# A kernel of linear attention and a dense layer: another order for all its steps

## The chip, the cores and the metric

The kernel runs on one core of one Trainium2 chip. A core has five engines with an instruction queue each: PE (TensorE, matmuls and transposes into the PSUM memory), DVE (VectorE), ACT (ScalarE, activation functions), POOL (GpSimd) and SP (SyncE, which issues DMA transfers here). Each queue is worked through strictly in order, and engines wait for each other through semaphores. PEld is the part of PE that loads weights ahead of the matmuls. The metric is the time of one execution on the device, in microseconds (us); smaller is better.

## The reference, cut to what matters

With x of 2048 tokens by 448 features, 16 heads of 28 and an inner width of 1792 (`split` and `merge_heads` stand for the reshapes):

```python
xn = _layernorm(x, axis=-1)
return x + _A_ref(xn, A_wqkv, A_w_phi, A_wo) + _B_ref(xn, B_w1, B_b1, B_w2)

def _A_ref(x, wqkv, w_phi, wo):          # H = 16, Dh = 28
    q, k, v = split(x @ wqkv)
    pq = jnp.einsum("bhsd,hdf->bhsf", q, w_phi)
    pk = jnp.einsum("bhsd,hdf->bhsf", k, w_phi)
    phi_q = jnp.concatenate([_softmax(pq, axis=-1), _softmax(-pq, axis=-1)], axis=-1)
    phi_k = jnp.concatenate([_softmax(pk, axis=-1), _softmax(-pk, axis=-1)], axis=-1)
    kv = jnp.einsum("bhsf,bhsd->bhfd", phi_k, v)
    z  = jnp.einsum("bhsf->bhf", phi_k)
    num = jnp.einsum("bhqf,bhfd->bhqd", phi_q, kv)
    den = jnp.einsum("bhqf,bhf->bhq", phi_q, z)[..., None] + 1e-6
    return merge_heads(num / den) @ wo

def _B_ref(x, w1, b1, w2):
    h = jnp.einsum("bsd,df->bsf", x, w1) + b1
    sp = jnp.log1p(jnp.exp(-jnp.abs(h))) + jnp.where(h > 0, h, jnp.zeros_like(h))
    return jnp.einsum("bsf,fd->bsd", h * jnp.tanh(sp), w2)
```

Everything up to `kv` and `z` needs all tokens; only then can any output of the attention be made. The dense layer (`_B_ref`) needs only the normalised x and is free to lie anywhere.

## The kernel before

**One list sets the order.** The whole kernel is a table of named steps, each of which appends instructions to the queues of the engines that it uses. A string named `ORDER` (L147) lists all step names; `run_order` calls them in that order. So the place of a name in the list fixes the place of each of its instructions in the queue of its engine. Waits follow from what each instruction reads and writes (`Program.op` and `Program.resolve`); a list that is legal gives the same numbers whatever its order. An instruction that waits holds up all that stands behind it in its queue.

**Tiles and pairs.** The 2048 tokens are 16 tiles of 128; two tiles make a pair (0 to 7). Most steps are named by a letter, a pair or tile, a part and an engine letter (`d` DVE, `a` ACT, `p` POOL, `m` DMA, `b` ACT and DVE together, `t` ACT tile by tile):

- `lx0s` to `lx6s` load x (tiles 0-1, 2-3, 4-5, 6-7, 8-11, 12-15; L270), `lkm`, `lkt`, `lvm` the weights of k and v (L273, L281), `lqT0` to `lqT3` the weights of q, transposed by the DMA on the way (L285), `lpa` the feature weights, `lbs` the bias, `l1m0` to `l1m2` and `l1t` the first dense weight (L277), `l2s` the second (L305), `los` the output weight (L312). The last letter is the issuing queue, `s` for SP and `a` for ACT.
- `st` statistics of a tile (L467 and L468 on DVE, or three activations on ACT), `rs` the reciprocal deviation of a pair (on ACT, or two instructions on POOL, L473 and L476), `xn` the normalised pair (three instructions on DVE, L501; or a small shift on DVE, L489, and three instructions on POOL, L496), `xt` its transpose: on PE with a copy out of PSUM (L509, L514 for ACT and L516 for DVE), or as a DMA from SP (`m`, L521). A DMA transpose of this kind also waits until tiles 0 and 15 of x have landed.
- `wtk`, `wmk`, `wmq` fold the feature weights into the weights of k and q (L561, L585); `qd` is a DVE copy that needs all four `lqT` (L289), and `wmq` needs `qd`.
- `v`, `k`, `q` of a pair are 14 matmuls each in two halves (part 1 has 8, part 2 has 6; `pair_part`, L438). Behind the second half, `v` is copied out of PSUM (DVE or ACT), `k` and `q` leave through two exponentials on ACT, of plus and of minus (L623, L684). `e` of a tile is the DMA transpose of the exponentials of q (L692); they lie in three buffers, so that pair u+3 waits for the `e` of pair u.
- `kn` of a pair and sign: a sum and a reciprocal on DVE (L631, L633) and a multiplication on POOL (L635). `kv` of a pair adds its 16 matmuls into one bank (L652); the first starts after any pair, the last needs all. `kvz` masks the sum (L664) and turns it by a DMA.
- `f1.3` and the like are the first dense matmul, of token half 1 and chunk 3 of 14; each is 14 matmuls in two halves (also L438) and a Mish activation on ACT (L703).
- `nd` of a tile: 16 small matmuls for numerator and denominator (L726) and seven instructions on DVE (L741 to L752); `ot` the DMA transpose of the result (L761).
- `G` and `wo` of a pair: the second dense matmul and the output matmul, in halves (`pair_out`, L866); for the last pair `g14`, `g15`, `wo7F`, `wo7H` (L828, L844). The last of them adds x (`finish`, L793). `sto` and `stt` store.
- `z16` is 16 matmuls on constants at the start (`warm`, L376), `pm pp pk pi pw bd pv` fill constants on POOL; `pp` is three memsets of gaps in the buffers of q.

**PSUM** has eight banks. `take2` and `take1` hand out the pair or the bank that was used longest ago, in the order of the list; so another order also gives other banks, and other waits for the engine that empties them.

**The stretches** of the order: loads and normalisation of the first pairs; `v k q` of all pairs with `kn` beside them; six `f` and the eight `kv`; the other 22 `f` with `nd` between them; then `G` and `wo` with the last `nd`; stores at the end.

Of the kernel before, what the change touches and what calls it, by code (L numbers as in the profile page):

```python
# [168 lines left out]
def _kernel(es, nc, A_x, A_wqkv, A_w_phi, A_wo, B_w1, B_b1, B_w2, out):  # L169
    def sb(name, shape, dtype):  # L170
        return es.enter_context(nc.sbuf_tensor(name, shape, dtype))

# [94 lines left out]


    def load_x(a, b, eng):
        dma(eng, lambda e: e.dma_start(x_all[:, a:b, :], x2[:, a:b, :]), w=[("x", t) for t in range(a, b)], tag="ldx")  # L270
# [235 lines left out]
    def transpose7(e, b, src, cut=7):  # L506
        for c in range(7):
            to = bank16(b)[:, c * P:(c + 1) * P] if c < cut else bank16(b + 1)[:, (c - cut) * P:(c - cut + 1) * P]
            ins = e.transpose(to, src[:, c * P:(c + 1) * P], ident[:])  # L509
        return ins  # L510

    def evac(eng, dst, src, r, w, tag):
        if eng == "ACT":
            op("ACT", lambda e: e.activation(dst(), src(), ACT.Copy), r=r, w=w, tag=tag)  # L514
        else:
            op("DVE", lambda e: e.tensor_copy(dst(), src()), r=r, w=w, tag=tag)  # L516
# [492 lines left out]
```

## Time and profile before

| what | value |
|---|---|
| median of 3 runs | 153.88 us (153.58, 153.88, 154.25) |
| the profiled execution | 154.01 us, with a span of 152.1 us |
| granted clock of PE in it | 1.0 |
| busy: PE, DVE, ACT, POOL | 145.4, 102.4, 74.1, 41.4 us |
| DMA | 17.24 MB, mean 113 GB/s |

The span runs from the first instruction of the profile to the last; the execution's time has some 2 us more around it. The profile is one execution. Its page gives totals; the trace behind it gives a timeline for each engine, what each engine's idle time waited for, and the chain of work that ended last. In a row of a timeline the columns are the start and the length in us, engine, line of the kernel, operation, what is written and read, shape and count, and in brackets the idle time ahead of it with what ended it; instructions of one kind that follow each other are merged. "SPq" is SP's queue issuing a DMA, and the length there is that of the issue. PE is pipelined: the ends of matmuls are modelled, so the distance between starts tells more than the length. In the chain of waits, the columns are start, length and engine with line.

### The profile page before, as it was taken

To read this page: it belongs to the slowest core of one execution; us is meant where nothing else is said; L and a number is where in the kernel's file an instruction comes from. 1 tells how busy PE (TensorE), PEld (TensorE's weight loads), DVE (VectorE), ACT (ScalarE), POOL (GpSimd) and SP (SyncE) were. 2 spreads that over 40 slices of the span, in tenths; PEclk is the share of its full clock that TensorE was granted. 3 is DMA by queue.
4 is the path that set the end of the run, shared out by engine and by line. 5 is a ranking of instruction groups with operands and counts; after the bars stand their busy time and mean duration, and the time that the engine had idled before them with its cause. 6 is when DMAs were issued, how large, how long until landed. Compare 5 with 4: busy or idle time off the path is not lost.

```text
span 152.1 us, 4002 instructions
## 1 busy us (share of the span) xinstructions
PE 145.4 (96%) x1735; PEld 76.1 (50%) x1735; DVE 102.4 (67%) x224; ACT 74.1 (49%) x96; POOL 41.4 (27%) x59
## 2 busy tenths in 40 slices
PE   7799997999899999999989999999999999999993
PEld 3475543556455584445434445444555555554552
DVE  0997999999999503059998378999373377252452
ACT  3889989796979994776756387100000000000000
POOL 7704743799899970000000000000000000000000
PEclk9999999999999999999999999999999999999999
DMA  5999759989999998840913510803300016003025
GB/s 136 294 136 337 156 166 161 251 158 136 198 190 173 251 271 207 157 89 0 98 37 59 39 26 0 65 2 65 60 0 4 16 49 181 0 4 60 0 100 201
DMA packets 39997, 17.24 MB, mean 113 GB/s; under 512 B 33964, under 2 KB 39212, under 8 KB 39980
## 3 DMA queue, kind: packets, MB, share of 16 engines
q1 hardware_dynamic: 39372, 16.87, 53.5%
q8 instruction: 13, 0.21, 0.6%
q10 hardware_dynamic: 608, 0.12, 0.4%
q14 instruction: 4, 0.03, 0.1%
HBM read 7.02 MB, written 1.84 MB: 58 GB/s over the span
## 4 chain that ended last, share of the span: by engine, by line
PE 69%; DVE 18%; SPq 6%; DMA 3%; ACT 2%; issue 1%
PE PS L438 32%; PE PS L866 28%; DVE stats L467 4%; PE PS L828 3%; SPq L285 3%; DMA x_all<-in_A_x_dram 3%; DVE v_all L745 3%; DVE v_all L747 2%; PE PS L652 2%; PE PS L726 2%; DVE v_all L749 2%; DVE xn L752 2%; DVE v_all L516 1%; DVE mv L468 1%; ACT actT L684 1%
## 5 line engine op out<-in xcount | busy, mean ns | idle before, releaser
L438 PE MATMUL PS<-xnT,W 64*128 64x512 bf16 x392 | 44.9, 376 | 0.9 <-ACT actT L623 0.5
L866 PE MATMUL PS<-W,actT 64*128 64x448 bf16 x392 | 38.7, 349 | 0.0
L703 ACT ACTIVATE actT<-PS,b1T 128x1024 bf16<-128x1024 f32 x28 | 29.8, 1113 | 13.4 <-PE PS L438 13.3
L438 PEld LDWEIGHTS PS<-xnT,W 64*128 64x128 bf16 x392 | 18.9, 94 | 21.7 <-DVE v_all L747 0.9
L866 PEld LDWEIGHTS PS<-W,actT 64*128 64x128 bf16 x392 | 18.8, 94 | 17.2
L635 POOL TENSOR_TENSOR actT<-actT,rSk 128x896 bf16<-128x896 bf16 x16 | 26.6, 1702 | 1.9 <-DVE rSk L633 1.3
L793 DVE TENSOR_TENSOR x_all<-PS,x_all 128x448 bf16<-128x448 f32 (+1 forms) x16 | 9.1, 615 | 15.8 <-PE PS L866 15.1
L631 DVE TENSOR_REDUCE Sk<-actT 128x32 f32<-128x896 bf16 x16 | 16.8, 1047 | 0.2
L741 DVE COPY Sq<-PS 128x16 f32<-128x16 f32 x32 | 4.0, 167 | 17.1 <-PE PS L726 17.0
L623 ACT ACTIVATE actT<-PS 128x896 bf16<-128x896 f32 x16 | 13.7, 923 | 1.0 <-PE PS L438 0.9
L438 PE MATMUL PS<-Wpk,xnT 64*128 64x448 bf16 x112 | 12.9, 350 | 1.0 <-DVE rSk L633 0.8
L438 PE MATMUL PS<-Wkv,xnT 64*128 64x448 bf16 x112 | 12.6, 349 | 0.0
L438 PE MATMUL PS<-Wpq,xnT 64*128 64x448 bf16 x112 | 12.5, 349 | 0.0
L467 DVE BATCH_NORM_STATS2 stats<-x_all 128x6 f32<-128x448 bf16 x14 | 8.5, 607 | 4.3 <-DMA x_all<-in_A_x_dram 4.3
L749 DVE TENSOR_TENSOR v_all<-v_all 128x464 f32<-128x464 f32 x16 | 10.3, 642 | 0.6
L745 DVE TENSOR_TENSOR v_all<-PS,Sq 128x464 f32<-128x464 f32 x16 | 10.3, 641 | 0.5
L752 DVE TENSOR_TENSOR xn<-v_all,rden 128x448 bf16<-128x448 f32 x16 | 10.0, 625 | 0.6
L747 DVE TENSOR_TENSOR v_all<-PS,Sq 128x464 f32<-128x464 f32 x16 | 10.1, 630 | 0.0
L684 ACT ACTIVATE actT<-PS 128x896 bf16<-128x896 f32 x10 | 8.6, 912 | 1.4 <-PE PS L438 1.4
L438 PEld LDWEIGHTS PS<-Wpk,xnT 64*128 64x128 bf16 x112 | 5.5, 94 | 5.8 <-DVE rSk L633 1.2
L438 PEld LDWEIGHTS PS<-Wpq,xnT 64*128 64x128 bf16 x112 | 6.0, 94 | 4.8
L438 PEld LDWEIGHTS PS<-Wkv,xnT 64*128 64x128 bf16 x112 | 5.8, 94 | 4.8 <-issue 0.6
(88 smaller groups left out, 128.8 us busy)
## 6 DMA issues: line engine op xcount, KB each, us to landing
W<-in_B_w_dram SPq DMA_DIRECT2D x1, 1568.0 KB, 7.5
out_dram<-x_all SPq DMA_DIRECT2D x7, 224.0 KB, 2.1
W<-in_B_w_dram SPq DMA_DIRECT2D x3, 448.0 KB, 4.2
x_all<-in_A_x_dram SPq DMA_DIRECT2D x4, 224.0 KB, 3.8
x_all<-in_A_x_dram SPq DMA_DIRECT2D x2, 448.0 KB, 4.2
Wkv<-in_A_wqkv_dram SPq DMA_DIRECT2D x2, 336.0 KB, 4.6
Wo<-in_A_wo_dram SPq DMA_DIRECT2D x2, 336.0 KB, 5.0
W<-in_B_w_dram SPq DMA_DIRECT2D x2, 224.0 KB, 4.8
```

Of the source, the lines that this page charges most:

```text
L438: ins = e.matmul(o, lhs(c, k), rhs(c, k), start=part == "1" and c == 0, stop=part == "2" and c == 2)
L467: op("DVE", lambda e: e.bn_stats(stats[:, t, :], x_all[:, t, :]), r=[("x", t)], w=[("st", t)], tag=f"bn{t}")
L623: op("ACT", lambda e, s=s: e.activation(E_of(u)[:, s, :, :], two(b, D), ACT.Exp, scale=1.0 if s == 0 else -1.0), r=[pb(b), pb(b + 1)], w=[ ...
L631: op("DVE", lambda e: e.tensor_reduce(Sk[u][:, s, :], Eh(), AX.X, ALU.add), r=[("E", u, s)], w=[("Sk", u, s)], tag=f"Sk{u}.{s}")
L635: op("POOL", lambda e: e.tensor_tensor(Eh(), Eh(), ap_on(rSk[u][:, s, 0:1], [[1, 2 * H], [0, DH]]), ALU.mult), r=[("E", u, s), ("rSk", u, ...
L684: op("ACT", lambda e, s=s: e.activation(Eq_of(u)[:, :, s, :].rearrange("p i (h n) -> p i h n", n=64)[:, :, :, 0:QP], two(b, D).rearrange(" ...
L703: op("ACT", lambda e: e.activation(actT[:, fc, q * 1024:(q + 1) * 1024], bank(b, 2), ACT.Mish, bias=b1T[:, fc:fc + 1]), r=[("b1T",), pb(b) ...
L745: op("DVE", lambda e: e.tensor_tensor(tv(t1[i]), num(0), sx(1), ALU.mult), r=[pb(b), pb(b + 1), ("Sq", i, 1)], w=[("t1", i)], tag=f"ta{t}")
L747: op("DVE", lambda e: e.tensor_tensor(tv(t2), num(1), sx(0), ALU.mult), r=[pb(b), pb(b + 1), ("Sq", i, 0)], w=[("t2",)], tag=f"tb{t}")
L749: op("DVE", lambda e: e.tensor_tensor(t1[i], t1[i], t2, ALU.add), r=[("t1", i), ("t2",)], w=[("t1", i)], tag=f"tc{t}")
L752: op("DVE", lambda e: e.tensor_tensor(o_sb[(t // 2) % 2][:, t % 2, :].rearrange("p (h d) -> p h d", d=DH), t1[i][:, :, 0:DH], ap_on(rden[i ...
L866: ins = e.matmul(bank(places[par][0])[:, 0:D], l, r, start=fresh[par], stop=places[par][2] and i >= len(todo) - 2)
```

## The change

The list is replaced by another that does the same work. Beside their order, these steps change engine or form:

| work | before | after |
|---|---|---|
| matmuls on constants | 16 | 12 |
| x tiles 0-1 (`lx0`) | issued by SP, after all other x | issued by ACT, before `x6` in the list |
| bias load and its turn (`lbs`, `b1`) | among the `q` steps | at the start, ahead of `x2` |
| `lx6` (x tiles 12 to 15) | behind the four `lqT` | ahead of the four `lqT` |
| statistics of tiles 5 and 15 | ACT, DVE | DVE, ACT |
| `rs` of pairs 2 and 6 | ACT | POOL |
| `xn` of pair 2 | POOL | DVE |
| `xt` of pair 3, of pair 1 | both, DVE | ACT, both |
| copy behind `wtk1` | both | DVE |
| copies behind `wmq0` | ACT | DVE |
| copy of `v`: ACT has pairs | 7, 4, 5 | 3, 1, 6, 0 |
| `pv` (POOL memset) | before the first `wmk` | between the first multiplications of `kn` |
| `pp` (POOL memsets) | one step | three steps, same order |

(`wmq0b` has no split form, so it runs on DVE alone.) The last steps are `g15 stt14 stt15` instead of `sto6 stt15`, in another order of the last `G`, `wo` and stores.

```diff
 ORDER = """
-pm pw lx3s pp pk lx1s lkms lkts st6d lpa table pi st7a st2d st3d rs3t xn3d lvms rs1a z16 xn1d bd wtk0b wtk1b lx2s xt3b
-pv xt1d wmk0b wmk1a lqT0 st5a st4d lqT2 rs2a v31a lqT1 lqT3 qd lx6s v11a lx4s v32d wmq1a lx0s k11 xn2p st15d st14d st10d
-l1m0s wmq0a st8d rs7p k12 xn7p st1d st9d k31 xt2m q11 l1m1s k32 v12d rs4p st12d xt7m st11d q31 q12 q32 q21 xn4d rs5p
-st13d v21d rs6a q22 xn5d st0d xt4m k21 xt5m v22d v71a k22 v72a rs0p k71 l1m2s k41 kn3.1 e3 k72 k42 xn6d v41a v51a ep e4
...
-f0.22 q71 kn2.0 q01 q72 l2s f0.11 f1.01 kn6.1 q02 f1.02 kn6.0 f0.12 kn4.1 kv2 kv3 kv5 kv1 kv4 kn0.0 kn0.1 kv6 kv0 kv7
-f1.131 f1.71 f0.51 kvz f0.81 f1.72 f0.52 f0.82 f1.132 f1.81 f0.131 f1.82 nd3 e15 f1.11 e1 e0 f0.132 f1.12 f1.121 nd2
-f1.91 f1.122 nd0 f0.101 f1.92 f0.71 f0.102 nd1 f0.72 f1.41 f0.01 ot1m nd6 e14 f1.42 f0.02 f0.91 f0.31 f0.92 ot0m nd7
...
+pm pw lx3s pp1 pp2 pp0 pk lx1s lkms lkts st6d lpa table pi st7a st2d st3d rs3t xn3d lvms rs1a xn1d lbs z12 lx2s lx0a
+lx6s wtk0b xt3a wtk1d bd xt1b lqT0 st5d b1 wmk0b st4d lqT1 wmk1a lqT3 lqT2 lx4s v31a v11d st15a st14d l1m0s v32a rs2p
+st13d qd k31 xn2d xt2m v12a rs7p xn7p wmq0b st0d st8d wmq1a l1ts k32 k11 q11 k12 st9d st10d xt7m rs4p st1d xn4d rs0p q12
+st11d q31 v21d q32 st12d xt4m q21 v22d rs5p k21 e3 xn5d rs6p xt5m q22 e2 k22 k71 v71a k72 xn6d xn0p kn3.0 pv v72d kn7.0
+xt0m k41 q41 k42 xt6m q42 l1m1s v41d k51 kn3.1 kn1.0 v42d l1m2s e7 k52 k01 kn1.1 e6 v61d k02 k61 e9 v62a v01d e5 k62
...
+e10 f1.22 f1.02 f0.22 f1.51 q71 e8 f1.52 q01 q72 f0.81 kn2.1 kn0.1 q02 kn4.1 kv2 kn4.0 e15 kv7 kv3 kv5 kv0 kv6 kv1 e14
+kv4 f0.82 f0.11 f0.101 f0.12 kvz f0.102 f0.71 f1.131 los f0.72 f1.132 nd2 l2s f0.121 e0 f0.41 f0.122 nd3 f0.42 f1.81
+f1.121 ot1m f1.82 f1.122 f0.111 nd6 f0.51 f0.112 e1 f0.52 f0.01 f1.71 f0.131 nd7 f1.72 f0.132 f0.02 f1.111 f0.91 f1.112
+nd0 f0.92 f0.31 f0.61 nd1 f1.61 ot3m f0.62 f0.32 f1.62 f1.101 f1.41 f1.102 wo32 ot0m f1.42 nd10 G31 nd11 f1.91 wo31 nd4
+f1.92 f1.11 G32 nd5 G12 ot5m nd14 ot2m f1.12 nd12 G11 wo01 wo11 G02 nd15 nd13 G01 wo12 wo21 G21 wo02 G62 ot6m wob sto1
...
+g15 stt14 stt15
 """
...
-    def p_pads():
-        for i in (1, 2, 0):
+    def p_pads(which):
+        for i in which:
...
+    for i in range(3):
+        add(f"pp{i}", p_pads, (i,))
```

More of the change, by code (lines that the diff above doesn't have):

```diff
@@ L147 @@
 ORDER = """
-pm pw lx3s pp pk lx1s lkms lkts st6d lpa table pi st7a st2d st3d rs3t xn3d lvms rs1a z16 xn1d bd wtk0b wtk1b lx2s xt3b
-pv xt1d wmk0b wmk1a lqT0 st5a st4d lqT2 rs2a v31a lqT1 lqT3 qd lx6s v11a lx4s v32d wmq1a lx0s k11 xn2p st15d st14d st10d
-l1m0s wmq0a st8d rs7p k12 xn7p st1d st9d k31 xt2m q11 l1m1s k32 v12d rs4p st12d xt7m st11d q31 q12 q32 q21 xn4d rs5p
-st13d v21d rs6a q22 xn5d st0d xt4m k21 xt5m v22d v71a k22 v72a rs0p k71 l1m2s k41 kn3.1 e3 k72 k42 xn6d v41a v51a ep e4
-k51 xn0p v42a xt6m kn7.0 e2 k52 v52a kn1.1 xt0m kn7.1 kn5.0 v61a lbs q41 v62d kn4.0 k61 q42 e5 e6 l1ts v01d kn2.1 k62
@@ L153 @@
-q51 v02d e7 q52 kn1.0 k01 b1 e10 k02 q61 kn3.0 f1.21 e9 q62 e11 f1.22 f1.31 f0.21 e12 e8 f1.51 e13 f1.32 f1.52 kn5.1 los
-f0.22 q71 kn2.0 q01 q72 l2s f0.11 f1.01 kn6.1 q02 f1.02 kn6.0 f0.12 kn4.1 kv2 kv3 kv5 kv1 kv4 kn0.0 kn0.1 kv6 kv0 kv7
-f1.131 f1.71 f0.51 kvz f0.81 f1.72 f0.52 f0.82 f1.132 f1.81 f0.131 f1.82 nd3 e15 f1.11 e1 e0 f0.132 f1.12 f1.121 nd2
-f1.91 f1.122 nd0 f0.101 f1.92 f0.71 f0.102 nd1 f0.72 f1.41 f0.01 ot1m nd6 e14 f1.42 f0.02 f0.91 f0.31 f0.92 ot0m nd7
-f0.32 f0.41 wob f1.101 f0.111 f0.42 f0.61 f1.102 f0.112 nd5 f0.62 f1.111 nd4 f0.121 f1.112 f1.61 f0.122 wo01 f1.62 ot3m
@@ L158 @@
-ot2m nd11 nd13 G02 wo11 wo32 nd12 G01 nd10 G11 wo22 wo02 ot6m ot5m G31 wo21 nd15 wo31 G21 G32 G12 wo12 sto1 G62 nd14 nd9
-G61 wo51 wo61 G51 G22 ot7m G42 sto0 sto3 nd8 ot4m wo52 G41 wo7F g14 wo62 wo7H wo41 G52 stt14 wo42 sto2 g15 sto5 sto4
-sto6 stt15
+pm pw lx3s pp1 pp2 pp0 pk lx1s lkms lkts st6d lpa table pi st7a st2d st3d rs3t xn3d lvms rs1a xn1d lbs z12 lx2s lx0a
+lx6s wtk0b xt3a wtk1d bd xt1b lqT0 st5d b1 wmk0b st4d lqT1 wmk1a lqT3 lqT2 lx4s v31a v11d st15a st14d l1m0s v32a rs2p
+st13d qd k31 xn2d xt2m v12a rs7p xn7p wmq0b st0d st8d wmq1a l1ts k32 k11 q11 k12 st9d st10d xt7m rs4p st1d xn4d rs0p q12
@@ new lines @@
+st11d q31 v21d q32 st12d xt4m q21 v22d rs5p k21 e3 xn5d rs6p xt5m q22 e2 k22 k71 v71a k72 xn6d xn0p kn3.0 pv v72d kn7.0
+xt0m k41 q41 k42 xt6m q42 l1m1s v41d k51 kn3.1 kn1.0 v42d l1m2s e7 k52 k01 kn1.1 e6 v61d k02 k61 e9 v62a v01d e5 k62
+kn2.0 q61 v02a q51 e4 q62 q52 v51d kn0.0 e13 kn5.1 ep kn7.1 f1.31 kn6.0 v52d kn6.1 e11 f1.32 f0.21 f1.21 kn5.0 e12 f1.01
+e10 f1.22 f1.02 f0.22 f1.51 q71 e8 f1.52 q01 q72 f0.81 kn2.1 kn0.1 q02 kn4.1 kv2 kn4.0 e15 kv7 kv3 kv5 kv0 kv6 kv1 e14
+kv4 f0.82 f0.11 f0.101 f0.12 kvz f0.102 f0.71 f1.131 los f0.72 f1.132 nd2 l2s f0.121 e0 f0.41 f0.122 nd3 f0.42 f1.81
@@ new lines @@
+f1.121 ot1m f1.82 f1.122 f0.111 nd6 f0.51 f0.112 e1 f0.52 f0.01 f1.71 f0.131 nd7 f1.72 f0.132 f0.02 f1.111 f0.91 f1.112
+nd0 f0.92 f0.31 f0.61 nd1 f1.61 ot3m f0.62 f0.32 f1.62 f1.101 f1.41 f1.102 wo32 ot0m f1.42 nd10 G31 nd11 f1.91 wo31 nd4
+f1.92 f1.11 G32 nd5 G12 ot5m nd14 ot2m f1.12 nd12 G11 wo01 wo11 G02 nd15 nd13 G01 wo12 wo21 G21 wo02 G62 ot6m wob sto1
+nd9 wo22 wo52 wo61 nd8 wo51 ot4m G61 G41 wo62 G51 G42 sto0 ot7m G52 G22 wo41 wo7F sto2 g14 wo42 sto5 sto3 sto6 sto4 wo7H
+g15 stt14 stt15
@@ L269, in load_x @@
     def load_x(a, b, eng):
-        dma(eng, lambda e: e.dma_start(x_all[:, a:b, :], x2[:, a:b, :]), w=[("x", t) for t in range(a, b)], tag="ldx")
+        dma(eng, lambda e: e.dma_start(x_all[:, a:b, :], x2[:, a:b, :]), w=[("x", t) for t in range(a, b)], tag=f"ldx{b - a}")
     def load_main(eng, name, dst, src):
@@ L529, in xT @@
             evac("ACT", lambda: xnT[:, u, 0:3, :].rearrange("p c n -> p (c n)"), lambda: bank16(b)[:, 0:3 * P], [pb(b)],
-                 [("xnT", u)], f"xTe{u}")
+                 [("xnT", u)], f"xTh{u}")
             evac("DVE", lambda: xnT[:, u, 3:7, :].rearrange("p c n -> p (c n)"), lambda: bank16(b + 1)[:, 0:4 * P],
@@ L951, in _kernel @@
     add("qd", double_qT)
-    for n, fn in (("pi", p_ident), ("pm", p_mask), ("pw", p_wbd), ("pv", p_ones), ("pk", p_mask2), ("pp", p_pads)):
+    for n, fn in (("pi", p_ident), ("pm", p_mask), ("pw", p_wbd), ("pv", p_ones), ("pk", p_mask2)):
         add(n, fn)
+    for i in range(3):
+        add(f"pp{i}", p_pads, (i,))
     for n in (4, 8, 10, 12, 14, 16, 18, 20):
```

## The prediction

> **What bounds the kernel now.** I read the page first, then the chain of waits that ended last, then the timeline of each engine. PE (the matmul engine) is busy 96% of the span; the view of waits, for PE alone, lists what its recorded idle time waited for (columns: total us, times, longest us).
>
> ```profile
> span 152.1 us, 4002 instructions
> ...
> PE 145.4 (96%) x1735; PEld 76.1 (50%) x1735; DVE 102.4 (67%) x224; ACT 74.1 (49%) x96; POOL 41.4 (27%) x59
> ...
> PE PS L438 <- DVE rSk L633: 0.8, 1, 0.8
> ...
> PE PS L726 <- DVE v_all L747: 0.6, 2, 0.4
> PE PS L438 <- ACT actT L623: 0.5, 1, 0.5
> PE PS L438 <- DVE v_all L747: 0.5, 1, 0.5
> PE PS L438 <- ACT actT L684: 0.2, 1, 0.2
> ```
>
> Only these 2.6 us lie inside the work; the rest of the 6.7 us of idle PE is the start and the end. A reordering leaves the matmuls as they are, so it can win little more than that, and can lose much more. The chain shows which engine paces which stretch.
>
> ```profile
> 9.74 3.94 DMA x_all<-in_A_x_dram
> ...
> 24.73 1.00 DVE Sk L631
> ...
> 26.23 12.03 PE PS L438 x125
> ...
> 41.70 12.46 PE PS L438 x118
> 54.16 3.27 PE PS L652 x128
> ```
>
> Up to 9.74 it is SP issuing transfers, to 13.7 an x load, to 26.2 DVE (the vector engine: statistics, normalisation), and from there PE almost alone, with DVE's `nd` chains in it at 69 to 80 and 94 to 99. One chain runs beside it, just off the path: the 16 multiplications of `kn` on POOL (GpSimd), which the last `kv` must wait for.
>
> ```profile
> 26.19 1.70 POOL L635 TENSOR_TENSOR actT<-actT,rSk 128x896 bf16<-128x896 bf16 x1 [1.34 <-DVE rSk L633]
> ...
> 28.72 1.74 POOL L496 TENSOR_SCALAR xn<-x_all,rstd,shift 128x448 bf16<-128x448 bf16 x3 [0.83 <-DVE shift L489]
> ...
> 40.92 14.95 POOL L635 TENSOR_TENSOR actT<-actT,rSk 128x896 bf16<-128x896 bf16 x9 [0.53 <-DVE b1T L516]
> ```
>
> POOL ends its 16th at 55.9; the `kv` matmuls run from 54.16 to 57.42. So POOL has about 1 us to spare, no more.
>
> **The change part by part.** No matmul of the result is added or removed. I walk the new order queue by queue, adding durations of rows.
>
> *The loads.* SP's issues and what the rings moved (0.375 us a slice, from 0):
>
> ```profile
> 4.06 0.49 SPq L270 DMA_DIRECT2D x_all<-in_A_x_dram  x1
> 4.59 5.11 SPq L285 DMA_TRANSPOSE WqT<-in_A_wqkv_dram  x4
> ...
> GB/s 0 0 0 0 29 172 231 253 347 308 265 330 375 261 256 206 246 272 373 347 283 121 121 209 258 6 66 184 56 143 76 239 382 363 354 392 401 311 344 349
> ```
>
> Now `x6` waits for four transposes, 1.26 us of SP each. After the change `lbs`, `lx2s` and `lx6s` come first, two issues of about 0.5 more, so the transposes start at 5.6 to 5.7 instead of 4.59. `qd` waits for the last of them until 11.37 (row in the next fence), so it lands at 11.3 now and some 1.1 us later then, at 12.4. Up to 7.9 us the row sums to 1.71 MB, which is all issued up to `x2`; `x6` (448 KB) then needs 1.3 us at 350 GB/s; with about 1 us to be confirmed it lands near 10, where it now lands at 13.68. `x0` moves to ACT's queue; that costs ACT an issue of about 0.4 us, as SP pays, in time in which it waits for PE anyway. Should `x6` and `x0` (0.69 MB) go wholly ahead of the transposes, these land 1.9 us later, at 14.3. I take 12.4: the rings are nearly empty at 9.4 in the row, so the transposes are limited by their issue. The Trainium skill, page "DMA: Bandwidth & Descriptors", section "Issuing engines are not separate DMA queues", says that DMAs of all issuing engines run on the same 16 engines and interleave, so that a second issuer saves issue time alone; by it `x0` takes its 0.6 us out of `x6`, which would land at 10.6; no run here shows it.
>
> *DVE up to the first `kn`.*
>
> ```profile
> 8.16 0.74 DVE L516 COPY Eq<-PS 112x512 bf16<-112x512 bf16 x2
> ...
> 9.69 0.61 DVE L516 CAST Wpk<-PS 128x448 bf16<-128x448 f32 x1
> ...
> 11.37 0.23 DVE L289 COPY WqT<-WqT 128x256 bf16<-128x256 bf16 x1 [0.33 <-DMA WqT<-in_A_wqkv_dram]
> ...
> 13.70 0.63 DVE L467 BATCH_NORM_STATS2 stats<-x_all 128x6 f32<-128x448 bf16 x1 [0.59 <-DMA x_all<-in_A_x_dram]
> ...
> 14.46 0.59 DVE L467 BATCH_NORM_STATS2 stats<-x_all 128x6 f32<-128x448 bf16 x1
> ...
> 20.62 0.86 DVE L501 TENSOR_SCALAR xn<-x_all,mv,rstd 128x448 bf16<-128x448 bf16 x3
> ...
> 23.68 1.06 DVE L516 CAST v_all<-PS 128x896 bf16<-128x896 f32 x1
> ...
> 26.03 2.18 DVE L501 TENSOR_SCALAR xn<-x_all,mv,rstd 128x448 bf16<-128x448 bf16 x3
> ```
>
> From 8.24, where both orders have normalised pairs 3 and 1, the new queue holds: three copies of PSUM (0.37, some 0.67 for the doubled one, 0.41), 11 statistics of 0.75, `b1e` 0.11, one cast 0.61, `qd` 0.23, four `xn` of 0.86 (`xn2` is new here, POOL's before), two shifts of 0.15, the two `wmq0` casts that were ACT's (1.22) and `ve2` 1.06: 16.7 us, so `kn3.0` starts at 25.0 if nothing waits. The doubled copy (112x1024) is in no row; it lies between one copy of 0.37 and two. Before, the same point (the shift of pair 0, for which POOL waits until 28.72) has `kn3.1` inside, the 1.4 us up to 26.03, and 0.4 of `ep` behind `xn6`: 28.7 less 1.8 is 26.9. The lead of 1.9 us is made of waits of 1.3 us up to 13.7, of `xn6`, which takes 2.18 us beside a POOL multiplication where others take 0.86 (no multiplication has begun by then in the new order), and of two `v` casts that go to ACT, less what DVE takes over. `qd` is reached at 13.4, after the transposes land. `wmq0`, queued in PE behind it, then starts at 13.7.
>
> POOL follows: `xn0p` from 25.0 to 26.7, 16 multiplications of 1.70 and the `pv` memset of 0.5 put among them: end 54.5, now 55.9.
>
> *PE up to `kv`.*
>
> ```profile
> 18.39 1.73 ACT L684 ACTIVATE actT<-PS 128x896 bf16<-128x896 f32 x2 [0.17 <-PE PS L438]
> ...
> 34.18 0.94 PE L438 MATMUL PS<-Wpk,xnT 64*128 64x448 bf16 x8
> ...
> 34.94 0.75 PE L438 MATMUL PS<-Wpq,xnT 64*128 64x448 bf16 x6
> ...
> 39.59 0.18 PE L697 MATMUL PS<-ident,b_rows 14*128 14x14 bf16 x1
> ...
> 41.70 1.04 PE L438 MATMUL PS<-xnT,W 64*128 64x512 bf16 x8 [0.48 <-ACT actT L623]
> ...
> 81.76 6.21 PE L438 MATMUL PS<-xnT,W 64*128 64x512 bf16 x56
> ...
> xnT<-xn SPq DMA_TRANSPOSE x6, 3.6
> ```
>
> By their starts 8 matmuls take 0.76 us, and 6 three quarters of that: a `v`, `k` or `q` of a pair (14) is 1.33 us, an `f` 1.5. At 26.23 ten and a half of the 24 are done. The new order: `v31` near 9.9 (`xTe1`, `b1` and two copies before it), then `v11 v32 k31 v12` to 13.3, a wait for `qd` to 13.7, both `wmq` 1.1, `k32 k11` to 16.1, then `q11` (its weights leave DVE at 15.9) and on without a gap, since `x2`'s transpose (`xn2d` done at 14.5, 3.6 to land) is there at 18.2 and wanted at 18.8. Nine are done at 23.4 and ten and a half at 25.5: 0.7 us won. Then ACT's 1.73 us for each `k` and `q` lags PE by some 2 us and stays so, as each second group is a `v` or another engine's. The `b1` step is now in the prologue (its 0.2 us won) and the wait of 0.48 at 41.70 falls away, as `f1.2` no longer takes the bank of a just finished `q`. `kv4`, the last, is reached at 54.6 and POOL ends at 54.5: no wait, no cover either. Each us by which DVE begins `kn3.0` later costs PE one.
>
> *After `kv`.*
>
> ```profile
> 72.47 0.25 DVE L741 COPY Sq<-PS 128x16 f32<-128x16 f32 x2
> ...
> 75.48 0.25 DVE L741 COPY Sq<-PS 128x16 f32<-128x16 f32 x2
> ...
> 110.73 8.11 PE L866 MATMUL PS<-W,actT 64*128 64x448 bf16 x84
> ...
> L703 ACT ACTIVATE actT<-PS,b1T 128x1024 bf16<-128x1024 f32 x28 | 29.8, 1113 | 13.4 <-PE PS L438 13.3
> ```
>
> An `nd` holds DVE 3.0 us, its banks 1.6. Before, some stand closer than that, and PE waits for L747, `nd`'s last reading of its banks, for 1.1 us (0.6 and 0.5 in the first fence). In the new order between two `nd`s lie at least two halves of `f`, mostly five or more, and from `nd10` on a `G` half of 2.65 us (28 of 84 in 7.94) nearly each time. Tight spots remain: `nd7` to `f1.11` 2.15 us for 1.8, `nd9` to `nd8` 1.9 for 1.8. I count 0.5 of the 1.1 as won, with 0 and 1.1 as ends. Mish on ACT (1.1 for 1.5 of PE) has room. SP issues `los` and `l2s` between `kvT` and `e0`; the one that waits is `nd0`, some 14 us later. The last steps are the old ones in another order; I take 0, within 0.3 either way.
>
> *The warm matmuls* are 12, not 16.
>
> ```profile
> 0.84 4.96 PE L376 MATMUL PS<-const-bfloat16-1.0 128*128 128x512 bf16 x16 [0.84 <-PEq L994]
> ...
> 3.67 1.63 PEld L376 LDWEIGHTS PS<-const-bfloat16-1.0 128*128 128x128 bf16 x8 [0.16 <-issue]
> ...
> 6.51 1.39 PE L561 MATMUL PS<-ident,Wkv 128*112 128x128 bf16 x16 [0.72 <-DMA Wkv<-in_A_wqkv_dram]
> ```
>
> Eight come in 2.9 us and eight in 1.6: the clock rises near 3.6. Twelve end near 5.0, and PE then idles 1.5 us, not 0.7, for a load that is the same. I count nothing, as both ends of the gap are fixed. The Trainium skill, page "TensorE: Matmul & The Clock Gate", section "Part 1: The HAM clock gate (the "warmup" mystery)", says that the clock is released after a busy window of about 3.4 us and falls back after an idle one; by it 1.5 us are too short to fall back; the trace has only the shorter gap of 0.7, after which the matmuls ran fast.
>
> **Sum**: 0.7 + 0.2 + 0.5 + 0.5 = 1.9 us won. The profiled execution took 154.01 us (span 152.1 and 1.9 around it), 0.13 above the median of the three runs, 153.88; taken from the median, 152.0 us.
>
> **The rivals.** (1) *DVE loses its lead* at a head-of-line wait (for `st5`'s load, `b1`, `qd` or `ve2`), and `kv4` waits for POOL. For it: DVE and POOL have no slack in the walk, and DVE already waited 1.3 us in this stretch. Against it: loads are earlier. With the 1.9 us lost POOL ends at 56.4 and `kv4` waits 1.8: 153.8, no change. (2) *The WqT transposes land late*, slower: PE is blocked at `wmq0` and DVE at `qd`, everything else behind them. It decides from 15.3: beyond it the 1.9 us are gone. Bounds: 12.4, and, with 0.69 MB ahead of them at the 125 GB/s of the slices in which they now run, 17.9; at 16.9 all is 3.5 us later: 155.5. Against it: 14.3 at the rate that x loads reach. (3) *The clock falls back* in the longer gap: the 3.4 us of matmuls from 6.5 to 9.9 run at 0.43 to 0.2 of the pace, at most 3.4 us more, of which 0.4 is the wait at `qd`; with about half on the path, 153.6, no change. (4) *New waits* in an order walked at full rate throughout: a bank, an `e` transpose (they are issued 1.3 us apart, up to just before `exq7`). 1 to 3 us spread: 153 to 155.
>
> **How the numbers follow.** Forecast 0.53, its own range 151.0 (all 2.6 us of waits and `b1`) to 153.0 (nothing in the prologue and after `kv`); (1) 0.17; (2) 0.12; (3) 0.05; (4) 0.13, shared as 0.05, 0.03 and 0.05 between the signs. A measurement of this kernel tells 0.5%, 0.8 us, from no change. Faster 0.58, same 0.25, slower 0.17. The range of 8 in 10 is 150.9 to 154.9.
>
> **What would show it.** Right: `x6`'s statistics without a wait before 12.7; first `kn` reduction near 25.0; POOL's last multiplication near 54.5; `kv` over near 55.3; PE waits behind `nd` under 0.6 us in all. Wrong: PE idle before `wmq0` past 14.3; DVE idle over 1 us between 8 and 25; PE waiting in `kv`; warm matmul pace lost after 6.5.

## The result and the profile after

| | median | executions | profiled execution, span |
|---|---|---|---|
| before | 153.73 us | 4, 153.22 to 154.25 | 154.01 us, 152.1 us |
| after | 151.23 us | 4, 151.12 to 152.13 | 151.12 us, 149.2 us |

The ratio is 0.9835, with a 95% interval of 0.9806 to 0.9865: 2.5 us, a gain of 1.65%. Measured again (experiment 10 below), the same kernel took 150.94 us (six executions, 150.63 to 152.19), ratio 0.9816 (0.9784 to 0.9849). A ratio, here and below, leaves out executions more than 1.5% above the fastest of their kernel, and is not the quotient of the medians beside it. The profiled executions differ by 2.9 us, of which this section gives an account.

The totals of the page after, and the view of PE's waits (total us, times, longest us):

```profile
span 149.2 us, 3996 instructions
...
PE 143.6 (96%) x1731; PEld 74.0 (50%) x1731; DVE 101.7 (68%) x226; ACT 73.5 (49%) x91; POOL 41.7 (28%) x60
...
PE PS L438 <- ACT actT L684: 1.3, 1, 1.3
```

The share of PE stands at 96% as before, and tells nothing. In the list of waits inside the work, everything is new: the waits for L631/L633 (`kn`), for L623 and for L747 (`nd`) are gone, and a single new one, of 1.3 us, has come: an exponential of q on ACT (L684) holds a bank. The chain of work that ended last shows where PE now paces alone, and where it does not:

```profile
6.74 0.63 PE PS L561 x8
...
14.05 18.66 PE PS L438 x196
...
38.13 3.56 DMA EqT<-actT
41.76 1.73 ACT actT L684 x2
43.54 8.87 PE PS L438 x84
52.41 3.27 PE PS L652 x128
55.67 6.93 PE PS L438 x62
```

PE alone is the pace from 6.74 to 32.71 (the rows between are of PE too), where it was from 26.23; its share of the chain rose from 69% to 86%. One foreign stretch is left before `kv`, from 32.7 to 43.5: two steps of ACT, SP's issues of `e`, the DMA transpose shown, then ACT. `kv` ends at 55.67, before at 57.42; the old order had the second half of an `f` (6 matmuls, 0.65 us) more done by then, so at equal work the lead is 57.42 - 0.65 - 55.67 = 1.1 us. The other 1.8 of the 2.9 us were won behind `kv`. (The expectations below have 1.0 and 1.9, counted with 7 matmuls.)

DVE and POOL up to there (timelines; start, length, engine, line, what, count, and in brackets the idle time ahead):

```profile
5.95 1.85 DVE L501 TENSOR_SCALAR xn<-x_all,mv,rstd 128x448 bf16<-128x448 bf16 x6
...
11.27 0.59 DVE L467 BATCH_NORM_STATS2 stats<-x_all 128x6 f32<-128x448 bf16 x1
...
12.80 0.23 DVE L289 COPY WqT<-WqT 128x256 bf16<-128x256 bf16 x1
...
23.57 1.08 DVE L631 TENSOR_REDUCE Sk<-actT 128x32 f32<-128x896 bf16 x1
```

```profile
43.34 9.98 POOL L635 TENSOR_TENSOR actT<-actT,rSk 128x896 bf16<-128x896 bf16 x6 [0.47 <-DVE rSk L633]
```

No brackets on DVE: neither the statistics of `x6` (11.27) nor `qd` (12.80) waits. The first reduction of `kn` begins at 23.57, and POOL's sixteenth multiplication ends at 53.3, 2.3 us before `kv` ends.

**The new wait, followed back.** ACT, PE and SP in the stretch that the chain pointed to:

```profile
41.76 1.73 ACT L684 ACTIVATE actT<-PS 128x896 bf16<-128x896 f32 x2 [1.87 <-DMA EqT<-actT]
```

```profile
43.54 4.71 PE L438 MATMUL PS<-xnT,W 64*128 64x512 bf16 x42 [1.28 <-ACT actT L684]
```

```profile
29.11 1.07 SPq L277 DMA_DIRECT2D W<-in_B_w_dram  x2
30.23 4.39 SPq L692 DMA_TRANSPOSE EqT<-Eq  x2
34.66 4.83 SPq L692 DMA_TRANSPOSE EqT<-actT  x3
```

The exponential of pair 5 writes the buffer of pair 2, so it waits for `e4`, the last of the three transposes issued from 34.66. Two `e` take 4.39 us of SP to issue, and three take 4.83, where one of them takes 1.3 alone. Just ahead stand the two large loads of W1. PE waits 1.28 us for the bank that the late exponential holds.

**Why the recorded waits are too small.** PE before, at two of the waits for `nd`, and PE after, at the same sequence without one:

```profile
74.24 2.54 PE L438 MATMUL PS<-xnT,W 64*128 64x512 bf16 x22
77.01 0.40 PE L726 MATMUL PS<-KVZ,EqT 56*128 56x60 bf16 x16 [0.23 <-DVE v_all L747]
77.24 2.32 PE L438 MATMUL PS<-xnT,W 64*128 64x512 bf16 x20
80.02 1.69 PE L438 MATMUL PS<-xnT,W 64*128 64x512 bf16 x14 [0.46 <-DVE v_all L747]
```

```profile
79.53 2.54 PE L438 MATMUL PS<-xnT,W 64*128 64x512 bf16 x22
81.91 0.28 PE L726 MATMUL PS<-KVZ,EqT 56*128 56x60 bf16 x8
```

From the start of 22 matmuls to that of the next row are 2.38 us where nothing waits (0.108 a matmul) and 2.77 us where 0.23 are recorded: the wait costs 0.39. The second costs 80.02 - 77.24 - 20 x 0.108 = 0.62, with 0.46 recorded. A pipelined matmul "ends" here 0.16 us after the next could start (79.53 + 2.54 against 81.91), and the bracket counts from that end. Counted so, the old order lost 0.39, 0.62, 0.56 (at 99.18) and, where nothing is recorded, 0.13 twice more (before 102.19 and 105.20): 1.8 us behind `kv`, not the 1.1 that are recorded. The new wait of 1.28 us costs 43.54 - 40.58 - 14 x 0.108 = 1.45 by the same rule.

### The profile page after: what moved, and what is told of

The parts are those of the page before. It is cut to its first block, busy times and chain, and to the rows that moved or that the text cites. A ratio compares the mean times of both kernels' runs of the same rounds, so it can differ in the third digit from the quotient of the medians.

```text
span 149.2 us, 3996 instructions
## 1 busy us (share of the span) xinstructions
PE 143.6 (96%) x1731; PEld 74.0 (50%) x1731; DVE 101.7 (68%) x226; ACT 73.5 (49%) x91; POOL 41.7 (28%) x60
## 4 chain that ended last, share of the span: by engine, by line
PE 86%; DMA 6%; ACT 3%; SPq 2%; DVE 1%; issue 0%; ACTq 0%
PE PS L438 44%; PE PS L866 31%; PE PS L828 3%; DMA Wkv<-in_A_wqkv_dram 3%; PE PS L726 2%; DMA EqT<-actT 2%; PE PS L652 2%; SPq L692 2%; PE PS L585 1%; ACT actT L684 1%; ACT actT L623 1%; PE PS L844 1%; PE PS L561 1%; ACT v_all L514 1%; SPq L270 1%; PE PS L509 1%
## 5 line engine op out<-in xcount | busy, mean ns | idle before, releaser
L438 PEld LDWEIGHTS PS<-xnT,W 64*128 64x128 bf16 x392 | 18.1, 94 | 22.5 <-ACT actT L684 1.8
L631 DVE TENSOR_REDUCE Sk<-actT 128x32 f32<-128x896 bf16 x16 | 16.7, 1043 | 0.0
L741 DVE COPY Sq<-PS 128x16 f32<-128x16 f32 x32 | 4.0, 167 | 15.8 <-PE PS L726 15.8
L623 ACT ACTIVATE actT<-PS 128x896 bf16<-128x896 f32 x16 | 13.7, 923 | 0.9 <-PE PS L438 0.8
L749 DVE TENSOR_TENSOR v_all<-v_all 128x464 f32<-128x464 f32 x16 | 10.3, 642 | 0.6
L745 DVE TENSOR_TENSOR v_all<-PS,Sq 128x464 f32<-128x464 f32 x16 | 10.3, 641 | 0.5
L747 DVE TENSOR_TENSOR v_all<-PS,Sq 128x464 f32<-128x464 f32 x16 | 10.1, 630 | 0.0
L684 ACT ACTIVATE actT<-PS 128x896 bf16<-128x896 f32 x10 | 8.6, 920 | 2.2 <-DMA EqT<-actT 1.9
L438 PEld LDWEIGHTS PS<-Wpq,xnT 64*128 64x128 bf16 x112 | 5.5, 94 | 5.2
```

The costliest lines, as they stand in the source:

```text
L438: ins = e.matmul(o, lhs(c, k), rhs(c, k), start=part == "1" and c == 0, stop=part == "2" and c == 2)
L623: op("ACT", lambda e, s=s: e.activation(E_of(u)[:, s, :, :], two(b, D), ACT.Exp, scale=1.0 if s == 0 else -1.0), r=[pb(b), pb(b + 1)], w=[ ...
L631: op("DVE", lambda e: e.tensor_reduce(Sk[u][:, s, :], Eh(), AX.X, ALU.add), r=[("E", u, s)], w=[("Sk", u, s)], tag=f"Sk{u}.{s}")
L684: op("ACT", lambda e, s=s: e.activation(Eq_of(u)[:, :, s, :].rearrange("p i (h n) -> p i h n", n=64)[:, :, :, 0:QP], two(b, D).rearrange(" ...
L745: op("DVE", lambda e: e.tensor_tensor(tv(t1[i]), num(0), sx(1), ALU.mult), r=[pb(b), pb(b + 1), ("Sq", i, 1)], w=[("t1", i)], tag=f"ta{t}")
L747: op("DVE", lambda e: e.tensor_tensor(tv(t2), num(1), sx(0), ALU.mult), r=[pb(b), pb(b + 1), ("Sq", i, 0)], w=[("t2",)], tag=f"tb{t}")
```

## The experiments

In the diffs the list is broken at the changed places. The moved names are shown where they arrive, not always where they left. "Before" in each comparison is the old kernel, measured beside it on the same chip. A time without an interval is one execution.

**1 and 2: half of the change each.** The new list up to the last `kv` with the old one behind it, and the reverse:

```diff
 ORDER = """
...
 e14 kv4 f0.82
-f0.11 f0.101 f0.12 kvz f0.102 f0.71 f1.131 los f0.72 f1.132 nd2 l2s
+los l2s f0.11 f0.12 f1.131 f1.71 f0.51 kvz f1.72 f0.52 f1.132 f1.81
...
```

> The new list up to the last kv (with f0.8 finished behind it), then the old list for everything after kv. Theory A (what is won in front of kv and what is won behind it add up): by the two traces the end of kv is 1.0 us earlier at equal work, so the time is about 152.7 us against 153.7 before, and the PE waits behind nd (L747) come back with 1.1 us recorded. Theory B (the part behind kv is paced by DVE or by loads, and a lead of PE at kv is lost there): 153.5 or more. Theory C (the part behind kv wins only because PE gets there earlier or with other banks): about 151.5.

```diff
 ORDER = """
...
-kv4 f0.82 f0.11 f0.101 f0.12 kvz f0.102 f0.71 f1.131 los f0.72 f1.132 nd2 l2s
+f1.52 kn5.1 los f0.22 q71 kn2.0 q01 q72 l2s f0.11 f1.01 kn6.1 q02 f1.02
...
+kn0.1 kv6 kv0 kv7 f0.81 e15 e14 f0.82 f0.101 kvz f0.102 f0.71 f1.131
...
```

> The old list up to the last kv, then the new list. Theory A: the stretch from the end of kv to the last matmul is 1.9 us shorter at equal work in the changed kernel, so about 151.8 us; no PE wait for L747 is left. Theory B' (only the 1.1 us of waits that the profile records as idle PE time are won): about 152.6 us.

The new front took 161.56 us against 153.87, ratio 1.0383 (1.0312 to 1.0455); the new back 153.57, ratio 0.9983 (0.9950 to 1.0015). Neither half wins what it wins in the whole. For the front, PE's waits, the chain, and windows (us; busy time of five engines; granted PE clock; share of the DMA engines; GB/s):

```profile
PE PS L726 <- DMA KVZ<-KVT: 5.4, 1, 5.4
```

```profile
61.52 9.46 DMA KVZ<-KVT
```

```profile
71.00:75.00 4.00, 3.88 (x34) 1.92 (x36) 2.96 (x7) 0.28 (x1) 0.00 (x0) 0.50 0.42 82
```

The small transpose of `kv` took 9.46 us to land, because in this splice it stands on SP behind `l2s`, the 1.57 MB of W2; before, W2 was loaded ahead of `kv`. PE waited 5.4 us, and then ran at half its clock for 6 us, the window shown and the time up to 77.2. The new back, in turn:

```profile
57.54 6.70 PE L438 MATMUL PS<-xnT,W 64*128 64x512 bf16 x56
64.89 0.40 PE L726 MATMUL PS<-KVZ,EqT 56*128 56x60 bf16 x16 [0.65 <-DMA KVZ<-KVT]
```

```profile
52.90 0.59 SPq L305 DMA_DIRECT2D W<-in_B_w_dram  x1
53.81 6.52 SPq L692 DMA_TRANSPOSE EqT<-actT  x2
60.37 2.32 SPq L670 DMA_TRANSPOSE KVZ<-KVT  x1
```

The first `nd` could have begun at 57.54 + 56 x 0.108 = 63.6; it begins at 64.89, since `kvT` stands behind `e15` and `e14`, and these behind W2. From this `nd` to the end of the last matmul stage there are 83.78 us in this run and 83.78 in the changed kernel, and no wait for L747 in either: the new back is worth its 1.8 us, and loses 1.3 of them at the seam.

**3 and 4: two mends for the seam.** The front of 1 with W2 behind `kvT`, and with W2 far ahead of it, as in the old list (the diffs are against 1):

```diff
 ORDER = """
...
-e14 kv4 f0.82 los l2s f0.11 f0.12 f1.131 f1.71 f0.51 kvz f1.72
+e14 kv4 f0.82 f0.11 f0.12 f1.131 f1.71 f0.51 kvz los l2s f1.72
...
```

> The new list up to the last kv and the old one behind it, as in the first experiment, but with the loads of Wo and W2 (los, l2s) behind the transpose of KVT on SP instead of ahead of it. Theory A (front and back add up; the first experiment was lost on KVT standing behind 1.57 MB of W2): about 152.7 us, with no PE wait for KVZ and 1.1 us of recorded PE waits for L747 (nd). Theory B (the lead of the new front is lost in the old back): 153.5 or more.

```diff
 ORDER = """
...
-q71 e8 f1.52
+q71 e8 los l2s f1.52
...
-e14 kv4 f0.82 los l2s f0.11
+e14 kv4 f0.82 f0.11
...
```

> The changed order up to the last kv, the old order behind it, with the two halves of W2 loaded right behind the transpose of e8, so ahead of kvT as in the old order. Theory A (the gains of the front and of the back add): the front brings 1.0 us, kv starts at 52.2 +- 0.3 and ends 1 us earlier than before, the recorded waits behind nd are back with 0.9 to 1.3 us, and the time is 152.7 (152.3 to 153.1) against 153.7. Theory B (the front hands kv over early, but the old back cannot use it, because W2 and the transposes stand in one queue): kv as by A, a wait of over 1 us for a transposed load between kv and the first nd, and 153.5 or more.

They took 156.50 us against 153.95, ratio 1.0186 (1.0139 to 1.0233), and 154.09 against 153.93, ratio 1.0005 (0.9979 to 1.0031). In the first the transposes `e1` and `e0` now stand behind W2, and an `nd` waits for them:

```profile
73.13 0.40 PE L726 MATMUL PS<-KVZ,EqT 56*128 56x60 bf16 x16 [2.49 <-DMA EqT<-Eq]
```

In the second no `nd` waits for a transpose. What PE waits for is ACT. Its profile is of the slowest of ten executions (155.05 us); ACT, then PE:

```profile
53.33 1.28 ACT L684 ACT_TABLE_LOAD   x1 [1.80 <-DMA EqT<-actT]
...
59.28 2.12 ACT L703 ACTIVATE actT<-PS,b1T 128x1024 bf16<-128x1024 f32 x2
```

```profile
60.45 1.83 PE L438 MATMUL PS<-xnT,W 64*128 64x512 bf16 x14 [0.69 <-ACT actT L703]
```

ACT waits for `e8`, reaches Mish at 59.28 (before: 56.53), its banks come free late, and PE waits 0.69 us at 60.45, 1.1 by starts (28 matmuls of `f` stand between 56.32 and there), which is the whole lead; the old waits for `nd` (L747) are there as well, with 1.1 us in the view of PE's waits. W2 is hardly the reason: `e8` lands 5.0 us after its issue here and 4.7 and 4.8 in 1 and 3, where W2 comes later, and the same wait stands in them too, with 0.43 and 0.52 us recorded. So the second theory held in the time (153.5 or more) and not in the place: what waited was an exponential on ACT, not an `nd`. The front's lead itself is there in 1 and 3, where the row behind `kv` starts at 55.48 and 55.35 (before: 57.35). Of the four splices three lose at the seam to a transpose on SP's queue behind W2, and the fourth to ACT, which comes late to Mish behind the new front. The gains of front and back are not parts that add; the new list, in which W2, `kvT`, the `e` and the `f` have other places, has neither loss.

**5 and 6: the new wait.** Is `e4` late because its turn in SP's queue is late, or because W1's loads stand ahead? In 5 the four `e` go ahead of W1; in 6 W1 goes behind `e4`.

```diff
 ORDER = """
...
-xt6m q42 l1m1s v41d
+xt6m q42 e5 e4 e7 e6 l1m1s l1m2s e9 e8 v41d
...
```

> The changed kernel with SP's queue reordered between xt6m and e13: e5 e4 e7 e6, then the two W1 loads, then e9 e8. Theory A (exq5 on ACT waits for e4, which was held up by two slow issues behind the W1 loads, and PE waits 1.28 us for its bank): the wait of ACT L684 for EqT near 42 and the PE wait of 1.28 us behind it go, and about 1.3 us are won against the changed kernel: about 149.9 us. Theory B (POOL is next: kv4 waits for the last phi): 0.5 us or less are won, with PE waiting in kv. Theory C (the W1 loads now land too late for f1.3): no gain, with PE waiting at the first f.

```diff
 ORDER = """
...
-xt6m q42 l1m1s v41d k51 kn3.1 kn1.0 v42d l1m2s e7
+xt6m q42 v41d k51 kn3.1 kn1.0 v42d e7
...
-q51 e4 q62
+q51 e4 l1m1s l1m2s q62
...
```

> The changed kernel with the two W1 loads l1m1 and l1m2 moved behind e4 on SP, nothing else. Theory A (SP's issues of e6 and e5 were slow, 3.10 and 2.08 us, since the rings held the W1 loads): all five e issues take about 1.3 us, e4 lands near 38, exq5 does not wait; f1.3 waits for W1 instead, by 1 to 2.5 us, so the time is within 1 us of the changed kernel. Theory B (they are slow for another reason, the buffer they read or PE and ACT traffic): the issues stay at 3.1 and 2.1 us.

5 took 151.53 us against 153.87, ratio 0.9836 (0.9796 to 0.9876): the same as the change. 6 took 153.15 in its one execution, more than the 1 us above the change that its theory A allowed. SP of 6, then PE of 6 and of 5:

```profile
29.70 2.70 SPq L692 DMA_TRANSPOSE EqT<-Eq  x2
32.45 4.14 SPq L692 DMA_TRANSPOSE EqT<-actT  x3
```

```profile
42.58 1.04 PE L438 MATMUL PS<-xnT,W 64*128 64x512 bf16 x8 [2.70 <-DMA W<-in_B_w_dram]
```

```profile
41.10 1.04 PE L438 MATMUL PS<-xnT,W 64*128 64x512 bf16 x8 [1.38 <-DMA W<-in_B_w_dram]
```

Without W1 ahead, the same five issues take 1.31 to 1.39 us each, so the loads in flight are what slows them. But then the first `f` waits for W1 itself, 1.38 or 2.70 us. The wait only changes its name: here the rings have too little time for both.

**7 and 8: W1 much earlier**, before the transpose of pair 7, and `e` ahead as in 5; the second also with the 16 warm matmuls of the old list, for a reason told below:

```diff
 ORDER = """
...
-st9d st10d xt7m
+st9d st10d l1m1s xt7m
...
-e3 xn5d
+e3 l1m2s xn5d
...
-xt6m q42 l1m1s v41d
+xt6m q42 e5 e4 e7 e6 e9 e8 v41d
...
```

> The changed kernel with SP's queue reordered: l1m1 ahead of xt7, l1m2 behind e3, and e5 e4 e7 e6 e9 e8 behind xt6. Theory A (the 1.28 us in which PE waits for exq5's bank are on the path and free once e4 and W1 are both early): no PE wait at the first f, about 149.9 us. Theory B (the transposes of xn5, xn0 or xn6 land later behind the W1 loads, and PE waits for them before v5, k5, k0 or v6): a wait of 0.5 to 1.3 us between 26 and 32 us, about 151 us. Theory C (POOL is next): PE waits for up to 0.5 us in kv.

```diff
 ORDER = """
...
-lbs z12 lx2s
+lbs z16 lx2s
...
```

> The order with l1m1 early, with 16 warming matmuls instead of 12. Theory A (the idle stretch ahead of the first Wk matmul lets the clock fall in some executions; longer warming closes it): wait ahead of the first q matmul under 1.0 us recorded, granted clock 1.00 in every run, 150.2 us (149.8 to 150.6), none above 151. Theory B (the fall has nothing to do with the idle stretch): runs spread from 150.3 to 152.1 as with 12.

They took 151.04 us (150.28 to 152.14), ratio 0.9808 (0.9769 to 0.9848), and 150.65 us (150.14 to 152.17), ratio 0.9802 (0.9761 to 0.9842). Both waits, for `e4` and for W1, are gone. Both intervals contain the change's own ratios, 0.9835 and 0.9816, so a gain beyond it is not shown. A profile of 8, its longest execution (152.17), has small new waits: for transposes of `xn`, which now stand behind W1, and for a reduction of `kn`:

```profile
PE PS L438 <- DMA xnT<-xn: 0.8, 3, 0.3
PE PS L438 <- DVE rSk L633: 0.6, 1, 0.6
```

In 7 the profiled execution (151.66 us) had another loss, at the start. PE, and then the windows:

```profile
6.93 1.06 PE L561 MATMUL PS<-ident,Wkv 128*112 128x128 bf16 x8 [2.01 <-DMA Wkv<-in_A_wqkv_dram]
```

```profile
7.00:8.00 1.00, 1.00 (x11) 1.00 (x11) 0.78 (x3) 0.00 (x0) 0.00 (x0) 0.50 1.05 368
...
9.00:10.00 1.00, 1.00 (x12) 1.00 (x11) 0.37 (x1) 0.69 (x1) 0.00 (x0) 0.50 0.83 98
```

After 2.01 us of idle PE the granted clock was 0.50 for 3.4 us (the window between them shows 0.50 too, and it is back at 10.4). Two of the six executions of 7 had a mean clock of 0.989 (151.66 and 152.14 us), four had 1.00 (150.28 to 151.29): by these six the fall costs about 1 us.

**9 and 10: are the 12 warm matmuls a gamble?** The changed kernel with 16, and once more as it is:

```diff
 ORDER = """
...
-lbs z12 lx2s
+lbs z16 lx2s
...
```

> The changed kernel with 16 warming matmuls instead of 12. Theory A (12 are a gamble on the clock): 151.1 us without runs above 151.5, so the median as with 12 and the spread less. Theory B (no influence): same median and same spread as with 12. If the 16 run into the Wk load, the first q matmul starts later and the time rises by up to 0.5 us.

> The changed kernel as it is, beside the three others. Theory A (12 are a gamble): most runs at 151.1 to 151.3 with clock 1.00, and one or two in ten at 152 with a lower mean clock. Theory B: all within 0.3 us of 151.2 at clock 1.00.

With 16: 151.51 us (150.73 to 151.93); with 12: 150.94 (150.63 to 152.19), all twelve at clock 1.00. The starts of 10 and of 9:

```profile
0.85 4.08 PE L376 MATMUL PS<-const-bfloat16-1.0 128*128 128x512 bf16 x12 [0.85 <-PEq L996]
6.73 0.62 PE L561 MATMUL PS<-ident,Wkv 128*112 128x128 bf16 x8 [1.81 <-DMA Wkv<-in_A_wqkv_dram]
```

```profile
0.85 6.42 PE L376 MATMUL PS<-const-bfloat16-1.0 128*128 128x512 bf16 x16 [0.85 <-PEq L996]
7.11 0.61 PE L561 MATMUL PS<-ident,Wkv 128*112 128x128 bf16 x8
```

In 10 PE idled 1.81 us and the clock stayed. In 9 the sixteen lasted until 7.27, past the landing of the load, and the first matmul of the kernel's own began 0.38 us later. So 16 do no measurable good and can cost some tenths; 12 leave a small chance of a fallen clock, which no execution of the changed kernel shows here. The spread of 1.2 to 1.6 us stays with either number, at clock 1.00, and what sets it is open; 8 too reached 152.17 with 16.

**11: `x6` behind the four `lqT` again**, as before the change:

```diff
 ORDER = """
...
-lx2s lx0a lx6s wtk0b
+lx2s lx0a wtk0b
...
-lqT3 lqT2 lx4s
+lqT3 lqT2 lx6s lx4s
...
```

> The changed kernel with the load of x tiles 12 to 15 put back behind the four WqT transposes. Theory A (the lead of the prologue comes from this load): it lands near 14, the first statistics of these tiles wait for it for 2.5 us or more on DVE and on ACT, the first kn starts near 26 instead of 23.6, and the time is 1.3 to 2.5 us above the changed kernel: 152.5 to 153.7. Theory B (the lead comes from the other order of DVE and the other engines): under 0.5 us more.

156.49 us against 153.95, ratio 1.0151 (1.0121 to 1.0181): 5.3 us above the change by the medians, more than either theory gave. PE, and the windows behind:

```profile
16.39 1.26 PE L585 MATMUL PS<-Wbd,WqT 112*128 112x112 bf16 x16 [3.10 <-DVE WqT L289]
```

```profile
16.00:18.00 2.00, 1.49 (x22) 1.06 (x24) 1.59 (x7) 2.00 (x5) 1.22 (x3) 1.00 0.07 27
18.00:20.00 2.00, 2.00 (x16) 0.79 (x14) 1.97 (x5) 2.00 (x4) 1.54 (x3) 0.55 0.73 129
```

The statistics of `x6` now stand in DVE's queue ahead of `qd`, so the whole queue waits for `x6`; PE waits 3.1 us for `wmq0`, and its clock falls, though not at once: it is still 1.00 from 16 to 18 (the 0.55 is a mean, with 0.50 from 18.5 on). The new DVE queue needs the early `x6`; what it wins against the old queue, which had `qd` ahead of these statistics, this run does not tell.

**12: the `pv` memset back to the start**, where the old list had it:

```diff
 ORDER = """
...
-xt3a wtk1d
+xt3a pv wtk1d
...
-kn3.0 pv v72d
+kn3.0 v72d
...
```

> The changed kernel with the POOL memset pv put back near the start, before PE's transposes of pair 1. Theory A (DVE's six xn instructions on pairs 3 and 1 were slowed by this memset): they take about 2.3 us again instead of 1.85, and the first kn starts 0.4 us later. Theory B: they stay at 1.85. The time is within 0.5 us of the changed kernel either way, as POOL ends its last phi half a us or more before the last kv wants it.

150.88 us in one execution. The memset and the six `xn` instructions in it, and before:

```profile
5.23 0.53 POOL L341 MEMSET v_all<- 128x256 uint32 x1
5.96 1.91 DVE L501 TENSOR_SCALAR xn<-x_all,mv,rstd 128x448 bf16<-128x448 bf16 x6
```

```profile
6.28 0.54 POOL L341 MEMSET v_all<- 128x256 uint32 x1
5.92 2.32 DVE L501 TENSOR_SCALAR xn<-x_all,mv,rstd 128x448 bf16<-128x448 bf16 x6
```

The changed kernel has 1.85. But the memset came too early here: it was over at 5.76, before the `xn` began, where in the old kernel it ran beside them. So the run does not try theory A, and what slowed them before stays open.

## Why the prediction was right, and where it was not

The forecast was 152.0 us with a range of 150.9 to 154.9. It came out at 151.23, on the side and in the range foretold. The sum was 1.9 us; the profiles show 2.9. By its own terms, the measured ones counted by starts:

| term of the sum | predicted | measured |
|---|---|---|
| prologue up to ten and a half groups | 0.7 | 1.64 |
| `b1` out of the `q` steps | 0.2 | 0.24, not tried alone |
| wait at 41.70 gone | 0.5 | 0.64 |
| new wait: `e4` | 0, a rival | -1.45 |
| waits for `nd` | 0.5 | 1.83 |
| sum | 1.9 | 2.9 |

That the total came so near is luck in part: the four gains were some 2.4 us larger than counted, and an unplanned wait of 1.45 us hid more than half of that.

- **The ceiling.** "Little more than 2.6 us" came from the recorded idle time and was too low: by starts, the old waits behind `kv` alone were worth 1.8. The prediction had itself noted that ends of matmuls are modelled and starts tell more, and yet took the bracket as the price.
- **The prologue: mechanism right, size off.** DVE paced the old start up to 26.2, and its new queue is shorter; in the new order the chain has no DVE between 6.74 and `kv`. That `x6` must be early for it, experiment 11 shows; the `v` casts on ACT were not tried alone. `kn3.0` began at 23.57, not 25.0. The mis-sized term is the DVE queue of 16.7 us from 8.24, which took 15.8 us from 7.80: durations were added where successive instructions overlap (statistics follow each other by 0.72 to 0.73 us, not 0.75), and the start, taken from the old row of six `xn` (2.32 us), was 0.44 late. Everything after followed: `wmq0` began at 13.09, not 13.7, and the two `wmq` took 0.9 us by starts, not 1.1; nine groups were done at 22.5, not 23.4; POOL's end was at 53.3, not 54.5.
- **The loads.** The second issue from 4.62 us, `x6`, took 4.8 us to land by the view of DMA issues, which puts it between 9.9 and 10.3, as predicted (near 10); ACT reads its tile 15 at 10.48 without a wait. `x0` was issued from ACT at 6.49, 0.36 us long. The Trainium skill, page "DMA: Bandwidth & Descriptors", section "Issuing engines are not separate DMA queues", says that DMAs of all issuers share the same engines; the estimate made from it was 10.6, a little late by this trace. DVE reaches `x6`'s statistics only at 11.27. `qd` did not wait, at 12.80 (predicted 13.4).
- **The wait at 41.70** is gone, as forecast. In the place that it held there is now **rival 4**, an `e` transpose, given a chance of 0.13. The step that missed it: "they are issued 1.3 us apart". That was read from the old `e` issues ahead of W2, none of which took over 1.57 us; behind W1's two loads a pair of them took 4.39 us. Its size varies: 1.28, 0.92 (experiment 12) and 0.41 us (experiment 10).
- **`kv` and rival 1.** POOL did not hold `kv`; it ended 2.3 us before it. DVE kept its lead. `kv` was over at 55.67, where 55.3 was expected: the early start had won 0.9 us more than counted, and `e4` cost 1.45.
- **Rival 2** needed the `lqT` to land after 15.3; `qd` ran at 12.80. What it feared, PE held at `wmq0`, is what experiment 11 built, and its price there, 5.3 us, was above the 3.5 assumed: `wmq0` began 3.3 us later than in the changed kernel, and the fallen clock behind it cost most of the other 2.0.
- **Rival 3**, the clock after a longer gap, did not happen in the changed kernel (gap 0.95 us recorded, and 1.81 in experiment 10), but did in its neighbour, experiment 7, at 2.01. The gap of 0.95 was luck: all twelve warm matmuls ran at the slow pace and ended at 5.8, not near 5.0. The price given, 1.6 us, is of the size of the 1 us seen there.
- **The `nd` stage.** No wait for L747 is left, where 0.5 of the 1.1 recorded us were counted as won. The two places called tight did not bind.

## What to carry to other kernels

A queue that issues both megabyte loads and small transposes on which engines wait is judged by what stands behind each large load: its small transposes wait for bytes, not for issues, so an order is moved as a whole or re-planned at every seam. The price of a wait on a pipelined engine is the distance between starts, less that of the same sequence without a wait; the recorded idle time is only its lower end. When a search offers a new order, walk the stretch behind every load with the issue times seen under load.

## What the runs showed of the hardware

- Issuing a transpose of `e` on SP took 1.23 to 1.39 us with little in flight. Two and three behind two loads of W1 (0.9 MB) took 4.39 and 4.83 us, two behind W2 6.52 (experiment 2). A transpose of `kv` issued behind 1.57 MB landed 9.46 us later (experiment 1).
- PE's granted clock fell to 0.50 after idle stretches of 2.01, 3.10 and 5.4 us, for 3.4, 3.4 and 6.8 us, and stayed at 1.00 after 0.95, 1.81, and also after 2.49 (experiment 3) and 2.70 us (experiment 6). Length alone does not decide between 2.0 and 2.7. The Trainium skill, page "TensorE: Matmul & The Clock Gate", section "Part 1: The HAM clock gate (the "warmup" mystery)", has a free-running window of 3413 ns, and a fall after one idle window. The stretches of 3.4 and 6.8 us at half clock are one and two such windows, and the dependence on the moment agrees with a free-running one. The fall after 2.01 us, less than a window, does not agree with a whole idle one: in experiment 7 the weight loads quicken at 3.6 and the clock falls at 6.9 to 7.0, one window later, though PE had worked up to 4.9.
- The same sixteen warm matmuls ended 4.96 us after their start before the change and 6.42 in experiment 9; the twelve took 4.94 in the changed kernel and 4.08 in experiment 10. Their weight loads come 0.43 us apart up to 3.4 before the change and in experiment 10, and up to 6.4 in experiment 9, and closer from there. So the moment at which PE turns fast varies by three microseconds from one execution to the next, though the granted clock reads 1.00 all the while.
